# A planned instruction order that puts attention ahead of the MLP on TensorE

## The chip, the cores and the metric

The kernel runs on one core of a Trainium2 chip. The metric is device time in microseconds for one execution, and the median of several runs is compared. A profile of one execution shows TensorE (PE, with its weight loads PEld), VectorE (DVE), ScalarE (ACT), GpSimd (POOL) and SyncE (SP), which issues most of the transfers.

## The reference, cut to what matters

Three layers follow each other on 3072 tokens (4 batches of 768): a linear recurrence ("attention"), an MLP, and a mixture of experts.

```
for t in range(S):                      # attention, 8 heads of 48, complex decay a
    S = a[t] * S + outer(k[t], v[t])    # real part is read
    y[t] = q[t] @ S.real
h = x @ w_in;  g = elu(h);  x = g @ w_out                 # MLP, 384 -> 2048 -> 384
logits = x @ w_gate + log1p(exp(x @ w_noise)) * noise     # routing, 8 experts
top2, weights = best two experts of each token
out[token] += weight * (relu(x[token] @ w1[e]) @ w2[e])   # experts, 384 -> 1024 -> 384
```

## The kernel before, in words

The recurrence is worked in 6 chunks of 128 time steps. A chunk has two units (12 in all, of two batches each). Attention for one unit: magnitudes and angles of the decay (`nat_a`), sums of angles over time by a triangular matmul (`tp<-tri`), cosines and sines on ACT (`X`), cumulative products (`E`), scaled keys and queries (`KK`, `X`), their scores `sc`, masked scores `P` on DVE, the output `py`, copied to `yr`, transposed and split into a high and a low part `xh`, `xl` (two buffers each, so two units of it can exist), and, for the next chunk, transposed keys `KT` and the state update `pu`. The sines need another ACT table than the exponentials, so each block of them has a table load before and after it.

The MLP for one unit works on `xh`, `xl` in 8 steps. A step has 18 matmuls into `ph` (first layer, high and low parts, 256 columns), five instructions on ACT and DVE (`ge`, `gh`, `gl`), and 12 matmuls into `y2` (second layer, shown as `y`). `ph` has two buffers. After the two units of a chunk the routing picks two experts for each token: small DVE and ACT instructions on one tile `route`, then matmuls into `pr` that rank the tokens of each expert, then 8 scatters from POOL's queue into `table`. `pr` uses the same two buffers as `ph`, in the order in which the program was written, so a `ph` tile that was written down after `pr` can't start before it.

The expert part then reads `slots` from the table (SP), gathers token rows `xr` (POOL), transposes them (`mtp`), and runs `mph` and `mpo` for expert after expert.

The order on each engine isn't the written one. `arrange` builds a list of all instructions with estimated costs and dependences and plays a list schedule: whichever engine is free first takes, of its ready instructions, the one with the best priority. It then fixes that order on every engine. Before, the priority is the length of the estimated chain that still hangs on the instruction (`tail`). Engines run their instructions in that fixed order; semaphores make them wait. The written order, set by the table `PAR` (class, start and length in units of time), matters through buffers, as with `pr`. Everything from the check on (`cut`, the end of routing and the experts) keeps its written order.

Of the kernel before, what the change touches and what calls it, by code (L numbers as in the profile page):

```python
# [10 lines left out]
F32 = mybir.dt.float32  # L11
# [10 lines left out]
PAR = {'EARLY': 8, 'x': (-0.25, 0.3), 'w': (0.15, 1.0), 'p': (-0.25, 0.6), 't': (-0.2, 0.0), 'o': (-0.1, 0.2), 'm': (0.35, 0.15), 's': (0.1, 0.0), 'k': (1.0, 0.0), 'v': (0.1, 0.0), 'a': (1.2, 0.55), 'b': (1.45, 0.35), 'f': (2.1, 0.95), 'r': (2.9, 1.05), ('pr', 'p'): 1.0, ('o', 1): 0.3, ('b', 2): -0.3, ('m', 's', 7): -0.1, ('t', 2): -0.3, ('b', 's', 8): 0.1, ('p', 's', 4): 0.2, ('a', 11): -0.15, ('b', 11): -0.3, ('b', 's', 11): 0.4, ('o', 11): -0.15, ('b', 's', 6): -0.1, ('a', 1): -0.15, ('p', 1): -0.3, ('p', 's', 3): 0.1, 'z': (0.9, 0.0), 'q': (0.3, 0.0), ('b', 's', 1): 0.1, ('p', 0): 0.3, ('o', 2): -0.3, ('a', 's', 0): -0.3, ('a', 's', 4): -0.5, ('a', 's', 6): 0.1, ('a', 's', 2): 0.1, ('k', 0): 0.15, ('o', 's', 0): -0.2, ('a', 0): -0.3, ('b', 's', 4): -0.2, ('b', 's', 0): 0.2, ('b', 's', 7): -0.3, ('m', 11): -0.3, ('b', 's', 2): 0.0, ('pr', 't'): -0.5, ('f', 2): 0.15, ('b', 's', 10): 0.3, 'ring': '0000001111', 'bufs': (2, 2), ('t', 0): -0.45, ('a', 's', 3): 0.1, ('p', 's', 0): -0.1, ('f', 0): -0.15, ('pr', 'q'): 0.5, ('b', 's', 12): -0.2, ('t', 1): 0.3, ('b', 's', 5): 0.3, ('m', 's', 0): 0.2, ('pr', 'f'): -0.5, ('pr', 'x'): -1, 'fs': 0, ('q', 0): 0.45, ('a', 's', 1): 0.1, ('k', 1): 0.15, ('o', 0): -0.3, ('m', 's', 8): -0.2, ('q', 2): -0.3, ('v', 0): 0.15, ('p', 2): 0.15}  # L22


def arrange(tc):


    nc = tc.nc
# [223 lines left out]
    pr = {h: -tail[h] if h < cut else 1e9 + h for h in heads}  # L252
# [6 lines left out]
    mode, dma, zeros = None, 0.0, []  # L259
# [22 lines left out]
    while done < len(heads):  # L282
# [15 lines left out]
        p, h = heapq.heappop(now[e])  # L298
        st = t
# [36 lines left out]
def tile_kernel(ctx, tc, q, k, v, a_re, a_im, w_in, w_out, w_gate, w_noise, noise, w1, w2, qp, kp, vp, ap,  # L336
# [33 lines left out]
    xs = dram.tile([N, Dm], F32, name="xs") if dbg is None else dbg["xs"]  # L370
# [512 lines left out]
    def route(lg, noi, tok, nt, small, psm, put):  # L883
# [45 lines left out]
        tt(both, oh[:, :, 0], oh[:, :, 1], op=OP.add)  # L929
        pr = psm()  # L930
# [26 lines left out]
    def r_pieces(c):  # L957
        def f():
            noi = wf.tile([128, B, E], F32, name="noi", tag="noi", bufs=1)
            nc.sync.dma_start(noi, noise.rearrange("(b t) e -> t b e", b=B)[c * L:(c + 1) * L])  # L960
            route(LG[c], noi, tokm[:, c, :], B, wf,
                  lambda: psf.tile([128, B + 1, E], F32, name="pr", tag="ph", bufs=2), put_row)
        return [(1.0, f)]
# [131 lines left out]
    def place(cls, u, pieces):  # L1095

        tot = sum(w for w, _ in pieces) or 1.0
        t0, ln = PAR[cls]
        if cls not in "wx":
            t0 += u + PAR.get((cls, u), 0.0)  # L1100
        t = 0.0
        for k, (w, f) in enumerate(pieces):
            t += w
            ev[cls, u, k] = [t0 + ln * t / tot + PAR.get((cls, "s", k), 0.0), f]

# [111 lines left out]
    settle(rules)  # L1217
    events = [(t, n, f, u, c) for n, ((c, u, k), (t, f)) in enumerate(ev.items())]
# [13 lines left out]
    for t, _, f, tag, cls in sorted(events, key=lambda e: e[:2]):  # L1232
        tc.cur_priority = int((t + 4 - PAR.get(("pr", cls), 0.0)) * SCALE)
        if dbg is not None:
            dbg["labels"].append((int(nc.get_next_instruction_name().split("-")[1]), f"{cls}.{kind(f)}:{tag}"))
# [3 lines left out]
    if dbg is not None and dbg.get("p1"):  # L1239
# [102 lines left out]
    def redo():  # L1342
# [79 lines left out]
        with tc.tile_pool(name="gf", bufs=1) as gf, tc.tile_pool(name="gfp", bufs=1, space=PSUM) as gp:  # L1422
# [20 lines left out]
            with tc.For_i(0, N, 128) as r:  # L1443
# [36 lines left out]
                route(lg, noi, tk, 1, gf, lambda: gp.tile([128, 2, E], F32, name="gfpr"), put)  # L1480
# [68 lines left out]
```

## Time and profile before

| | |
|---|---|
| median of 3 runs | 1263.4 us (1262.4 to 1264.09) |
| profiled execution, its own time | 1264.73 us |
| its span in the profile | 1262.9 us |
| PE busy | 1164.5 us, 92% |
| DVE busy | 791.2 us, 63% |
| ACT busy | 649.5 us, 51% |
| mean granted TensorE clock | 0.966 |

The start, to about 160 us, loads and splits weights. From 160 to about 767 us attention and MLP run interwoven; from then the experts run. In the middle part the same pattern comes back about every 112 us, once for each chunk.

### The profile page before, as it was taken

The page shows a single profiled execution, that of the slowest core. Times are in us where ns is not written, and L with a number is a line of the kernel's source. Part 1 is how long each engine was busy: PE and PEld are TensorE (multiplying, and loading weights), DVE is VectorE, ACT ScalarE, POOL GpSimd, SP SyncE. Part 2 cuts the span into 40 slices and gives each one's busy share as a digit, 9 for nine tenths or more (in the row PEclk, how much of TensorE's full clock was granted, in tenths as well). Part 3 has the DMA queues.
Part 4 walks back from the last instruction along what each step waited for, and adds up shares of the span by engine and source line. Part 5 has one row for each costly group of instructions (what it writes and reads, how often), then busy time and mean ns, then how long its engine had stood idle before and what let it go on. Part 6 is the DMA issues. An engine that isn't in the chain of part 4 may idle for free.

```text
span 1262.9 us, 22761 instructions
## 1 busy us (share of the span) xinstructions
PE 1164.5 (92%) x8821; PEld 1077.0 (85%) x8821; DVE 791.2 (63%) x1782; ACT 649.5 (51%) x1299; POOL 243.2 (19%) x265
## 2 busy tenths in 40 slices
PE   4786999889899989999997999799999999999997
PEld 3464989889898988989897998789898989898996
DVE  5799986996898699679848466343443343443221
ACT  6777766685766678576745374232323232332111
POOL 2110000030020003001100502433424242424222
PEclk9597999999999999999998999899999999999999
DMA  6455502211121111112100234343434342423111
GB/s 216 124 154 175 181 28 66 64 48 36 61 74 34 56 50 57 45 56 79 35 26 20 53 106 120 99 125 103 127 97 126 94 133 84 134 83 109 36 44 34
DMA packets 64309, 107.05 MB, mean 85 GB/s; under 512 B 19967, under 2 KB 46310, under 8 KB 64192
## 3 DMA queue, kind: packets, MB, share of 16 engines
q1 hardware_dynamic: 50096, 65.65, 17.5%
q0 software_dynamic: 14096, 39.86, 10.4%
q8 instruction: 71, 1.16, 0.4%
q14 instruction: 46, 0.38, 0.1%
HBM read 86.98 MB, written 20.70 MB: 85 GB/s over the span
## 4 chain that ended last, share of the span: by engine, by line
PE 59%; DVE 24%; ACT 10%; issue 4%; DMA 1%; POOL 0%; another core or an unknown queue 0%; SPq 0%; POOLq 0%; ACTq 0%; DVEq 0%
PE mpo L1073 17%; PE mph L1051 17%; PE y L859 8%; PE ph L835 8%; DVE E L618 2%; DVE ge L841 2%; DVE KK L677 2%; DVE X L686 2%; PE mtp L1036 1%; DVE gl L845 1%; DVE Sc L755 1%; ACT L562 1%; DVE P L768 1%; PE sc L764 1%; PE tp L587 1%
## 5 line engine op out<-in xcount | busy, mean ns | idle before, releaser
L1053 ACT ACTIVATE egh<-mph 128x320 fp32r<-128x320 f32 (+1 forms) x128 | 66.3, 518 | 231.6 <-PE mpo L1073 131.9
L951 POOL DMA_INDIRECT table<-route x48 | 55.1, 1148 | 613.1 <-DVE route L945 542.3
L1073 PE MATMUL mpo<-weh,egh 128*128 128x384 f32 (+1 forms) x448 | 151.7, 339 | 0.0
L1073 PE MATMUL mpo<-weh,egl 128*128 128x384 f32 (+1 forms) x448 | 151.6, 338 | 0.0
L1073 PE MATMUL mpo<-wel,egh 128*128 128x384 f32 (+1 forms) x448 | 151.2, 337 | 0.0
L859 PE MATMUL y<-woh,gh 128*128 128x400 f32 x384 | 141.0, 367 | 0.5 <-ACT yo L871 0.5
L859 PE MATMUL y<-woh,gl 128*128 128x400 f32 x384 | 132.6, 345 | 0.0
L859 PE MATMUL y<-wol,gh 128*128 128x400 f32 x384 | 131.4, 342 | 0.0
L1078 DVE SCALAR_TENSOR_TENSOR ac<-mpo,slots,ac 128x384 f32<-128x384 f32 (+1 forms) x49 | 30.2, 617 | 160.8 <-PE mpo L1073 160.8
L1054 DVE SCALAR_TENSOR_TENSOR egl<-mph,egh 128x320 fp32r<-128x320 f32 (+1 forms) x128 | 75.2, 587 | 87.1 <-ACT egh L1053 59.4
L835 PE MATMUL ph<-xh,wih 128*128 128x256 f32 x576 | 106.4, 294 | 4.0 <-DVE ge L841 3.9
L1004 ACT ACTIVATE weh<-raw 128x384 fp32r<-128x384 f32 x128 | 65.4, 523 | 86.6 <-PE mpo L1073 60.0
L835 PE MATMUL ph<-xl,wih 128*128 128x256 f32 x576 | 101.3, 285 | 2.8 <-DVE xl L802 2.7
L835 PE MATMUL ph<-xh,wil 128*128 128x256 f32 x576 | 100.7, 284 | 0.0
L1081 POOL DMA_INDIRECT out_dram<-ac,slots x56 | 55.4, 989 | 234.2 <-DVE ac L1078 210.5
L845 DVE TENSOR_TENSOR gl<-ge,gh 128x512 fp32r<-128x512 f32 x96 | 65.8, 689 | 49.3 <-ACT gh L844 48.6
L835 PEld LDWEIGHTS ph<-xh,wih 128*128 128x128 f32 x576 | 87.9, 191 | 5.6 <-PE sc L764 3.6
L844 ACT ACTIVATE gh<-ge 128x512 fp32r<-128x512 f32 x96 | 60.4, 629 | 61.4 <-PE y L859 49.4
L839 ACT ACTIVATE ge<-ph 128x512 f32<-128x512 f32 x96 | 57.2, 596 | 63.6 <-DVE gl L845 47.1
L835 PEld LDWEIGHTS ph<-xl,wih 128*128 128x128 f32 x576 | 83.0, 191 | 3.8 <-DVE xl L802 3.8
L841 DVE SCALAR_TENSOR_TENSOR ge<-ge,ph 128x512 f32<-128x512 f32 x96 | 65.6, 683 | 32.2 <-ACT ge L840 27.3
L1005 DVE TENSOR_TENSOR wel<-raw,weh 128x384 fp32r<-128x384 f32 x128 | 69.3, 556 | 25.8 <-ACT weh L1004 18.8
(207 smaller groups left out, 2861.7 us busy)
## 6 DMA issues: line engine op xcount, KB each, us to landing
raw<-in_moe_w_dram SPq DMA_DIRECT2D x128, 192.0 KB
nat_a<-in_a_rows_dram SPq DMA_DIRECT2D x24, 512.0 KB
raw<-in_moe_w_in_dram POOLq DMA_DIRECT2D x16, 384.0 KB
raw<-in_moe_w_out_dram POOLq DMA_DIRECT2D x16, 384.0 KB
q<-in_q_pairs_dram SPq DMA_DIRECT2D x24, 256.0 KB
k<-in_k_pairs_dram SPq DMA_DIRECT2D x24, 256.0 KB
vt<-in_v_rows_dram SPq DMA_DIRECT2D x24, 192.0 KB
out_dram<-zero SPq DMA_DIRECT2D x24, 192.0 KB
```

Of the source, the lines that this page charges most:

```text
L835: mm(ph[:, j, :], w[:, z, :], x[:, z, :], start=n == 0, stop=n == 3 * KD - 1)
L839: act(e, ph, AF.Relu, scale=-1.0)
L841: stt(e, e, -1.0, ph, op0=OP.add, op1=OP.max)
L844: act(gh, e, AF.Copy)
L845: tt(gl, e, gh.bitcast(F32), op=OP.subtract)
L859: mm(d["y"][i], g[:, j, i * L:(i + 1) * L], w, start=s == 0 and j == 0 and n == 0, stop=s == NS - 1 and j == 1 and n == 2)
L1004: act(w[0], raw, AF.Copy)
L1005: tt(w[1], raw, w[0].bitcast(F32), op=OP.subtract)
L1051: mm(ph[:, :n], w[:, z, :], x[:, z, :], start=k == 0, stop=k == 3 * KD - 1)
L1053: act(gs[0][:, f, :n], ph[:, :n], AF.Relu)
L1054: stt(gs[1][:, f, :n], ph[:, :n], 0.0, gs[0][:, f, :n].bitcast(F32), op0=OP.max, op1=OP.subtract)
L1073: mm(po[:m], x[:, f, o:o + m], w, start=k == 0, stop=k == 3 * FE - 1)
```

## The change

`arrange` gets two new rules. First, a PE instruction before `cut` that touches neither a `ph` nor a `y2` tile gets 30000 added to its priority, so that attention (and weight splitting, ranking and `mtp`) is taken ahead of any MLP matmul that is ready at that moment. Second, a sine block on ACT (an instruction with an estimated cost over 900 ns, after 150 us) is taken only when PE has at least 5000 ns of ready work by the estimate; after 12000 ns of waiting it is taken all the same. The routing becomes a generator in two pieces, `choose` (up to the two experts) and `rank` (from `pr` on), and for all chunks but the last it is written down later, in the midst of the next unit's MLP (in `PAR`, 'r' goes from (2.9, 1.05) to (2.5, 1.05), and `place` adds the chunk's number and 1). An empty list `ORDER` and some unused debugging lines change nothing.

```diff
-    pr = {h: -tail[h] if h < cut else 1e9 + h for h in heads}
+    pr = {}
+    for h in heads:
+        mlp = any(x[4] and x[0].startswith(("ph_", "y2_")) for x in acc[h])
+        pr[h] = 1e9 + h if h >= cut else -tail[h] - (30000 if eng[h] == "PE" and not mlp else 0)
...
+    hold = 5000
...
+        if hold and e == "Activation" and step[h] > 900 and t > 150000:
+            if free["PE"] - t + sum(work[x] for _, x in now["PE"]) + sum(work[x] for r, _, x in cand["PE"] if r < t) < hold:
+                waited.setdefault(h, t)
+                if t < waited[h] + 12000:
+                    nxt = min([free[x] for x in E if free[x] > t] + [t + 500])
+                    heapq.heappush(cand[e], (max(nxt, t + 100), p, h))
+                    continue
...
         tt(both, oh[:, :, 0], oh[:, :, 1], op=OP.add)
+        yield
         pr = psm()
...
-        return [(1.0, f)]
+        return [(1.0, choose), (0.3, rank)]
...
+        if cls == "r" and u < NC - 1:
+            t0 += u + 1
```

The instructions are the same in number and kind on all five engines; only their order differs. PE's order is the same up to the first MLP matmul (about 127 us in the trace) and again from the last 48 `y` matmuls on.

PE, just ahead of the ranking of chunk 2 (units count from 0, so chunk 2 has units 4 and 5). Before, this is the end of attention for unit 6, and no MLP matmul is among the rows:

```order
L786 MATMUL py<-vt,P 64x48 x2
L800 MATMUL tp<-ident,yr 128x128 x3
L711 MATMUL tp<-ident,KK 128x128 x8
L800 MATMUL tp<-ident,yr 128x128 x3
L725 MATMUL pu<-vt,KT 64x48 x16
L764 MATMUL sc_5438<-X,KK 128x128
L587 MATMUL tp<-tri,nat_a 128x128 x4
L933 LDWEIGHTS before
```

The changed kernel ahead of the same ranking; this is attention for unit 7, and `ph` and `y_5157`, `y_5158` belong to the MLP of unit 6:

```order
L801 MATMUL py<-vt,P 64x48 x2
L850 MATMUL ph<-xh,wih 128x256 x3
L850 MATMUL ph<-xl,wih 128x256 x3
L850 MATMUL ph<-xh,wil 128x256 x3
L815 MATMUL tp<-ident,yr 128x128 x3
L726 MATMUL tp<-ident,KK 128x128 x4
L874 MATMUL y_5157<-woh,gh 128x400
L874 MATMUL y_5157<-wol,gh 128x400
L874 MATMUL y_5157<-woh,gl 128x400
L874 MATMUL y_5158<-woh,gh 128x400
```

Before, the MLP of unit 5 has just been used up there, and the first matmul of unit 6's stands behind the ranking. Now attention is one unit further on at the same ranking, MLP matmuls of unit 6 stand between its steps, and 27 more `ph` matmuls of unit 6 follow the ranking.

PE, the first transposes for the experts (`mtp`), in the MLP of unit 10 (`y_7818` before, `y_7756` now). Before:

```order
L835 MATMUL ph<-xh,wih 128x256 x3
L835 MATMUL ph<-xl,wih 128x256 x3
L835 MATMUL ph<-xh,wil 128x256 x3
L1036 MATMUL mtp<-ident,xr_8129 128x128 x3
L1036 MATMUL mtp<-ident,xr_8131 128x128 x3
L859 MATMUL y_7818<-woh,gh 128x400
```

Now:

```order
L874 MATMUL y_7757<-woh,gl 128x400
L1059 MATMUL mtp<-ident,xr_8129 128x128 x3
L850 MATMUL ph<-xh,wih 128x256 x3
L850 MATMUL ph<-xl,wih 128x256 x3
L850 MATMUL ph<-xh,wil 128x256 x3
L1059 MATMUL mtp<-ident,xr_8131 128x128 x3
L850 MATMUL ph<-xh,wih 128x256 x3
L850 MATMUL ph<-xl,wih 128x256 x3
L850 MATMUL ph<-xh,wil 128x256 x3
L1059 MATMUL mtp<-ident,xr_8133 128x128 x3
```

What moved is the distance from the last ranking of chunk 4 (`pr`), on whose table rows the gathers wait: before, 198 `ph`, 84 `y` and 86 attention matmuls stand between its last matmul and the first `mtp`; now 81 `ph` and 42 `y` matmuls and nothing else. Behind the last attention matmul before the experts stood 153 `ph` and 150 `y` matmuls; now 351 and 276.

## Rows read from the trace of the kernel before

**Rows 1.** The page: span, and busy time of the engines.

```profile
span 1262.9 us, 22761 instructions
PE 1164.5 (92%) x8821; PEld 1077.0 (85%) x8821; DVE 791.2 (63%) x1782; ACT 649.5 (51%) x1299; POOL 243.2 (19%) x265
```

**Rows 2.** Busy time by stretch; behind the colon the stretch's length, then engines, clock.

```profile
160.00:222.80 62.80, 59.72 (x534) 57.45 (x534) 47.46 (x95) 42.70 (x83) 0.00 (x0) 1.00 0.16 47
222.80:334.68 111.88, 104.10 (x1036) 100.02 (x1035) 91.60 (x217) 77.45 (x151) 9.70 (x8) 0.98 0.18 53
...
446.49:558.29 111.80, 104.33 (x1036) 100.12 (x1035) 91.53 (x217) 77.19 (x149) 9.69 (x8) 0.98 0.18 53
558.29:674.60 116.31, 108.80 (x1083) 104.45 (x1081) 89.44 (x215) 70.70 (x131) 10.59 (x8) 0.97 0.16 43
674.60:730.00 55.40, 46.75 (x431) 45.51 (x432) 34.13 (x85) 25.85 (x43) 15.80 (x22) 0.91 0.17 48
```

**Rows 3.** Waits of PE from 222.8 to 674.6 us: total, times, longest.

```profile
PE tp L711 <- ACT KT L713: 12.0, 8, 2.4
PE py L786 <- DVE P L768: 9.1, 8, 1.8
PE ph L835 <- DVE ge L841: 3.9, 7, 0.8
PE ph L835 <- DVE xl L802: 2.7, 4, 0.7
PE pr L933 <- DVE route L929: 1.6, 2, 1.4
```

**Rows 4.** Timeline of PE, one chunk's stall: start, duration, [idle before, releaser].

```profile
452.37 0.32 PE L786 MATMUL py<-vt,P 128*64 128x48 f32 x4 [1.74 <-DVE P L768]
...
457.40 0.66 PE L711 MATMUL tp<-ident,KK 128*128 128x128 f32 x4 [0.83 <-ACT KT L713]
...
462.55 0.17 PE L933 MATMUL pr<-route,before 128*128 128x8 bf16 x1 [1.36 <-DVE route L929]
```

**Rows 5.** Busy time and granted clock by stretch, around two stalls.

```profile
450.00:452.30 2.30, 0.63 (x13) 0.43 (x12) 2.30 (x5) 2.27 (x4) 0.00 (x0) 1.00 0.00 0
452.30:454.60 2.30, 2.23 (x52) 2.23 (x52) 2.24 (x5) 0.49 (x3) 0.00 (x0) 0.66 0.28 46
454.60:457.40 2.80, 1.97 (x13) 1.48 (x11) 2.65 (x12) 1.76 (x6) 0.00 (x0) 0.67 0.34 126
...
683.00:688.40 5.40, 5.40 (x27) 5.40 (x27) 4.52 (x12) 1.72 (x3) 0.00 (x0) 0.50 0.10 36
```

**Rows 6.** Timeline of PE, the ranking of chunk 4.

```profile
682.50 0.17 PE L933 MATMUL pr<-route,before 128*128 128x8 bf16 x1 [7.30 <-DVE route L929]
```

**Rows 7.** Timeline of ACT, a sine block and the first instruction behind it.

```profile
494.56 1.28 ACT L562 ACT_TABLE_LOAD   x1
...
498.91 1.28 ACT L569 ACT_TABLE_LOAD   x1
500.21 0.63 ACT L844 ACTIVATE gh<-ge 128x512 fp32r<-128x512 f32 x1
```

**Rows 8.** Timelines: from ranking to first scatter, chunk 5.

```profile
777.45 0.17 PE L935 MATMUL pr<-route,ones 128*128 128x8 bf16 x1
779.53 1.02 POOL L951 DMA_INDIRECT table<-route  x1 [58.05 <-DVE flags L1272]
```

**Rows 9.** Timelines, chunk 4: first and last scatter, slots, first gather, first mtp.

```profile
700.73 0.96 POOL L951 DMA_INDIRECT table<-route  x1 [93.68 <-DVE route L945]
...
709.57 0.96 POOL L951 DMA_INDIRECT table<-route  x1 [0.31 <-issue]
711.91 0.39 SPq L1020 DMA_DIRECT2D slots<-table  x1
715.40 1.06 POOL L1031 DMA_INDIRECT xr<-xs,slots  x1 [1.92 <-DMA slots<-table]
734.81 0.82 PE L1036 MATMUL mtp<-ident,xr 128*128 128x128 f32 x6
```

**Rows 10.** Timelines: a later gather, and the mtp that waits for it.

```profile
795.01 1.05 POOL L1031 DMA_INDIRECT xr<-xs,slots  x1 [3.67 <-issue]
...
798.15 0.55 PE L1036 MATMUL mtp<-ident,xr 128*128 128x128 f32 x3 [1.40 <-DMA xr<-xs,slots]
```

**Rows 11.** Chain that ended last: start, length, what; one MLP step.

```profile
396.13 2.17 PE y L859 x12
398.30 2.14 PE ph L835 x18
```

More of the change, by code (lines that the diff above doesn't have):

```diff
@@ L25, in arrange @@
+ORDER = []
 def arrange(tc):
@@ L258, in arrange @@
     now = {e: [] for e in E}
-    mode, dma, zeros = None, 0.0, []
+    hold = 5000
+    mode, dma, zeros, waited = None, 0.0, [], {}
+    work = {h: sum(step[z] for z in members[h]) for h in heads}
     order = []
@@ L369, in tile_kernel @@
     nc.scalar.preload_act_table_set("natural_log_exp_and_others")
-    xs = dram.tile([N, Dm], F32, name="xs") if dbg is None else dbg["xs"]
+    xs = dram.tile([N, Dm], F32, name="xs")
     table = dram.tile([E * RS, 2], I32, name="table")
@@ L957, in r_pieces, with choose, rank @@
     def r_pieces(c):
-        def f():
+        g = []
+        def choose():
             noi = wf.tile([128, B, E], F32, name="noi", tag="noi", bufs=1)
             nc.sync.dma_start(noi, noise.rearrange("(b t) e -> t b e", b=B)[c * L:(c + 1) * L])
-            route(LG[c], noi, tokm[:, c, :], B, wf,
-                  lambda: psf.tile([128, B + 1, E], F32, name="pr", tag="ph", bufs=2), put_row)
-        return [(1.0, f)]
+            g.append(route(LG[c], noi, tokm[:, c, :], B, wf,
+                           lambda: psf.tile([128, B + 1, E], F32, name="pr", tag="ph", bufs=2), put_row))
+            next(g[0])
+        def rank():
+            for _ in g[0]:
+                pass
+        return [(1.0, choose), (0.3, rank)]
     def clear_table(pool):
@@ L1217, in tile_kernel @@
     settle(rules)
+    if ORDER:
+        for z, t in zip(ev.values(), ORDER):
+            z[0] = t / 5000.0
+        settle(rules)
     events = [(t, n, f, u, c) for n, ((c, u, k), (t, f)) in enumerate(ev.items())]
@@ L1231, in tile_kernel @@
             events.append((te, len(events), lambda f=f, n=n: e_weight(0, f, n), "m", "M"))
-    for t, _, f, tag, cls in sorted(events, key=lambda e: e[:2]):
+    for t, n, f, tag, cls in sorted(events, key=lambda e: e[:2]):
         tc.cur_priority = int((t + 4 - PAR.get(("pr", cls), 0.0)) * SCALE)
         if dbg is not None:
-            dbg["labels"].append((int(nc.get_next_instruction_name().split("-")[1]), f"{cls}.{kind(f)}:{tag}"))
+            dbg["labels"].append((int(nc.get_next_instruction_name().split("-")[1]), n, cls, tag, kind(f)))
         f()
     tc.cur_priority = (NU + 10) * SCALE
-    if dbg is not None and dbg.get("p1"):
+    if False:
         sm.close()
@@ L1479, in put @@
                                                  out_offset=bass.IndirectOffsetOnAxis(ap=idx, axis=0))
-                route(lg, noi, tk, 1, gf, lambda: gp.tile([128, 2, E], F32, name="gfpr"), put)
+                for _ in route(lg, noi, tk, 1, gf, lambda: gp.tile([128, 2, E], F32, name="gfpr"), put):
+                    pass
                 ts(tk, tk, 128.0, None, op0=OP.add)
```

2 lines of the change are left out of this document (1 added, 1 removed).

## The prediction

> **What bounds the kernel now.** I read the page first: TensorE is busy 92% of a span of 1262.9 us, VectorE 63% and ScalarE 51% [rows 1]. That is a mean over parts with different limits, so the next view is the busy time by stretch. From 222.8 to 674.6 us one pattern repeats four times, once a chunk; the third of these is alike to the second, which I left out. In each TensorE is idle for 7.8 us (111.88 less 104.10, 111.80 less 104.33; the last 116.31 less 108.80), while VectorE is busy 91.6 of 111.9 us and ScalarE 77 [rows 2]. So TensorE is nearest to its limit, VectorE has some 20 us of room in a chunk. Behind these four, 674.6 to 730 has 8.65 us of TensorE's idle time, and ahead of them 160 to 222.8 has 3.1 [rows 2].
>
> The view of waits says what the idle time of the four chunks is made of: 12.0 us for transposed keys that ScalarE copies, 9.1 for masked scores that VectorE makes, 1.6 for the ranking, all of them attention's chain or routing, and 6.6 for the MLP's own tiles, together 29.3 us [rows 3]. The timeline of one chunk shows where: within 12 us TensorE waits 1.74, 0.83 and 1.36 us [rows 4]. These stand in the piece of the order in which attention's steps follow each other without an MLP matmul between. They are not stalls of an engine that lacks speed, but of one that has nothing else ready: the MLP of the unit before is done, and the next needs `xh`, `xl` from the end of this very chain.
>
> Each such cluster costs twice. The granted clock behind the first gap is 0.66 and 0.67 for 5.1 us, after 2.30 us in which TensorE was busy 0.63 [rows 5]. TensorE was busy 4.2 us of these, and a third of that is 1.4 us a chunk. The ranking of chunk 4 is the longest wait of all, 7.30 us [rows 6], with matmuls of the next MLP queued behind it that need nothing from it but their turn in the `ph` buffers; then TensorE runs 5.4 us at 0.50 [rows 5], which is the lower of the two levels, 1.2 GHz, and loses 2.7 us.
>
> **The change part by part.** No instruction is added or removed, so nothing has a price of its own; the sum is made of gaps that close and gaps that open.
>
> *Attention first (A).* In the changed order attention runs about one unit ahead of the MLP, as far as two `xh` buffers let it, and MLP matmuls stand between its steps. The work that now hides attention's chain is the MLP of the unit before: a step of it is 2.14 and 2.17 us on TensorE [rows 11], eight steps a unit. In the changed order the second half of each unit's attention resumes just behind the last `ph` matmul of the MLP two units back, after a stretch of MLP alone. So attention waits for TensorE's MLP, no longer the other way, and a chain that is late has that stretch to catch up. The idle time of the four chunks is 30.5 us (7.8, 7.7, 7.5 and 7.5) [rows 2]. What can remain? Attention's matmuls are now put exactly where the planner thinks that they become ready, so each lateness of the chip against the planner is a stall with MLP matmuls queued behind it. The nearest row is the sine block: from the first table load to the next instruction it holds ScalarE 5.65 us [rows 7], and the rule asks for 5.0 us of work on TensorE, so at the end of each block TensorE lacks 0.65 us and then about the 0.63 us of ScalarE's next instruction, 1.3 us, twice a chunk. With 0.2 us for the rest I take 2.8 us a chunk. The gain is 30.5 less 11.2, 19.3 us; the bounds are 0 (all gaps come back elsewhere) and 30.5.
>
> *Clock (B).* 1.4 us in each of four chunks is 5.6. Gaps of 1.3 us are shorter than the 2.30 us one that pulled the clock down, but not absent; I take half, 2.8, between 0 and 5.6.
>
> *The hold on the sines.* It delays ScalarE's longest block until TensorE has work; what it saves is in A. It can cost: the sines wait up to 12 us, and scores of the next unit wait for them. The stretch of MLP alone hides that; if that cover is gone, the delay is in rival 2.
>
> *Routing split and shifted (C).* `pr` now takes its turn among the `ph` buffers in the midst of the next unit's MLP, so the chain of small VectorE instructions has several MLP steps of 4.3 us [rows 11] to end in. The wait of 7.30 us goes, and the slow 5.4 us behind it: 10.0 us, at least 7.3. The 1.6 us in the four chunks [rows 3] is already in A.
>
> *Early stretch (D).* Of 3.1 us from 160 to 222.8 I take 1.0; attention has no lead yet. Bounds 0 and 3.1.
>
> *The first transposes for the experts (E).* This is the loss. Chunk 4 is ranked later, and its table rows must land before the first gather. The chain: last ranking matmul to first scatter 2.1 us, with VectorE little loaded [rows 8]; first to last of eight scatters 8.84; to the slots' load 2.34; to the first gather 3.49 [rows 9]; from a gather to the transpose that waits for it 3.14 [rows 10]. Together 19.9 us. In the old order 52 us lay between ranking and `mtp` (682.50 to 734.81) [rows 6, 9]. In the new one 81 `ph` and 42 `y` matmuls do, 81/18 times 2.14 and 42/12 times 2.17 [rows 11], 17.2 us. And `mtp` is among the instructions that are taken first, so the MLP matmuls that could fill the gap stand behind it. That is a new wait of 2.7 us, with some 0.3 for VectorE's MLP instructions among the ranking's, and 1.4 us of slow clock as after the gap of similar length: 4.4 us lost, bounds 2.4 and 7. The next three `mtp` are 1.1 us of matmuls and 0.3 of their own apart, gathers come about every 1.3, so they add nothing.
>
> The MLP that is left when attention ends, 351 and 276 matmuls in place of 153 and 150, costs nothing: it is the same work later, and a stretch of MLP alone keeps TensorE busy without a gap [rows 11]. The experts' order is the same.
>
> The sum: 19.3 + 2.8 + 10.0 + 1.0 - 4.4 = 28.7 us. The profiled execution took 1264.7 us, so 1236.0; the runs' median, 1263.4, is 1.3 lower than that execution, which gives 1234.7, **1235 us**. The ends of the terms give 1264.7 - 46.8 = 1218 and 1264.7 - 0.3 = 1264 on the same footing, 1217 and 1263 for the median.
>
> **The rivals.**
>
> *1. The gaps move and don't close.* Attention's chain runs through VectorE and ScalarE; the order of these two isn't governed by the new rule. For it: VectorE is busy 82% of a chunk [rows 2], and attention must now be done sooner. By the order, the MLP alone behind the last attention grows by 198 `ph` and 126 `y` matmuls, 46 us [rows 11], and VectorE's work for attention must fit into that much less time. Against it: 20 us of its time are free in each chunk. Then A, B and D are nothing, and C less E is left, 5.6 us: about 1258. One rule of the Trainium skill points this way: "Perfetto Trace Analysis", section on optimization strategy, says that a gap that keeps repeating on the engine that should be full can mean too few buffers for the next tile. By that rule a new order gains nothing here until `xh` or `ph` get a third buffer, and the sum would be 1258; the trace agrees only for the ranking, which waits for its turn in the buffers, while the larger waits end on a copy or a masked score [rows 3], on data, not on a buffer.
>
> *2. Slower: in-order stalls.* A unit's attention has about 15 groups of matmuls, 30 a chunk, each now at its earliest place, with the MLP queued behind it. If each stalls by as much as an average MLP wait now, 0.6 us (6.6 us in 11 times [rows 3]), that is 18 us a chunk in place of 7.6: 42 us more over four chunks, less the 5.6 of C and E: about 1300. It decides from the point at which a group stalls 0.3 us on the mean: 9 us a chunk, so that 1.4 us more in each of four chunks eats the 5.6. Against it: the small waits now stand once or twice a chunk at places where filler was to be had, not at all of them, and lateness doesn't pile up over the stretch of MLP alone.
>
> *3. Nearly all gaps close*, and the clock stays up: 1264.7 - 46.8, about 1217.
>
> *4. No change*: what A gains, late groups take, within 2.5 us of 1263.4. I count a difference under 0.2%, 2.5 us, as one that these measurements can't tell from none.
>
> **How the numbers follow.** Forecast (A between 11 and 26, others near their values; 1225 to 1245): 0.60. Rival 1 (1248 to 1261): 0.18, of which 0.02 lies within the 2.5 us. Rival 2: 0.11. Rival 3: 0.07. Rival 4: 0.04. Faster: 0.60 + 0.16 + 0.07 = 0.83; same 0.06; slower 0.11. The range from 1219 to 1257 holds the forecast, most of rival 1 and most of rival 3, and leaves out rival 2, rival 4 and the ends, about 2 in 10.
>
> **What would show it.** Right: between about 200 and 640 us TensorE idle 3 us or less per 104 us of its work, the waits for `KT` and `P` at under half of [rows 3], no wait of `pr` over 1 us, the span of the experts the same, and a new wait of `mtp` for `xr` of about 3 us some 40 us before `mph` starts. Wrong for rival 1: the same waits in sum at other steps, VectorE busy over 95% where they stand. Wrong for rival 2: many waits of 0.3 to 1 us at `sc`, `py`, `KT` and `yr`, with a granted clock under 0.9 in the chunks. If `pr` still waits some us, the shift was too small and C is lost; if `mtp` waits 10 us, the ranking's chain was longer than from these rows.

## The result, and the profile after

The changed kernel takes 1252.4 us (median of 4 runs, 1249.1 to 1253.4), the kernel before 1262.9 us in the runs beside it: a ratio of 0.9915, 95% interval 0.989 to 0.9939. It is 10.5 us faster. The forecast was 28.4 us less than before: the direction was right and the time lies inside the range, but the gain is well under half of what the sum had.

The page of the changed kernel, span and busy time as in [rows 1]:

```profile
span 1251.6 us, 22832 instructions
PE 1160.8 (93%) x8821; PEld 1070.9 (86%) x8821; DVE 786.7 (63%) x1782; ACT 648.9 (52%) x1299; POOL 234.4 (19%) x265
```

Busy time of the changed kernel in the stretches of [rows 2], then up to the first expert matmul (`mph`), which starts at 757.0 us; behind the colon the stretch's length, then PE, PEld, DVE, ACT and POOL, and the granted clock:

```profile
160.00:222.80 62.80, 56.09 (x561) 53.01 (x560) 57.39 (x122) 42.69 (x82) 0.00 (x0) 0.97 0.17 55
222.80:334.68 111.88, 104.71 (x1125) 98.31 (x1123) 101.15 (x243) 86.02 (x173) 8.55 (x8) 1.00 0.21 68
334.68:446.49 111.81, 106.36 (x1106) 102.45 (x1105) 95.14 (x233) 78.93 (x156) 7.67 (x8) 0.98 0.18 55
446.49:558.29 111.80, 104.46 (x1030) 99.96 (x1029) 91.35 (x218) 76.91 (x149) 7.83 (x8) 0.97 0.17 53
558.29:674.60 116.31, 112.38 (x1028) 108.99 (x1027) 78.11 (x173) 62.34 (x105) 11.39 (x18) 1.00 0.10 31
674.60:757.00 82.40, 79.59 (x548) 78.34 (x547) 44.78 (x112) 46.47 (x94) 12.19 (x12) 1.00 0.25 73
160.00:757.00 597.00, 563.60 (x5385) 541.04 (x5384) 467.92 (x1096) 393.36 (x755) 47.62 (x54) 0.99 0.18 55
```

The same view of the kernel before, whose first `mph` starts at 766.5 us:

```profile
160.00:766.50 606.50, 564.28 (x5392) 544.20 (x5392) 470.51 (x1092) 396.64 (x757) 55.47 (x54) 0.98 0.19 54
```

Length less PE's busy time is TensorE's idle time. From 160 us to the experts it falls from 42.2 to 33.4 us, and the busy time by 0.7 us; that is the 9.5 us by which the experts start earlier, and the other 1.8 us of the span lie behind. The four chunks' stretches hold 23.9 us of idle time (7.2, 5.5, 7.3 and 3.9) where there were 30.5. These stretches are the same in time, not in work: the changed order does 4289 matmuls in the four, the old one 4191. Only the stretch from 160 us to the experts compares nearly the same work (5385 and 5392).

What these 23.9 us are made of, in the view of waits of the changed kernel over the same 222.8 to 674.6 us (total, times, longest), against [rows 3]:

```profile
PE ph L850 <- DVE ge L856: 6.8, 10, 2.1
PE pr L949 <- DVE route L944: 6.3, 3, 2.7
PE y L874 <- DVE gl L860: 3.1, 4, 0.9
PE py L801 <- DVE P L783: 1.9, 2, 1.2
PE sc L779 <- DVE sx L744: 1.8, 2, 1.0
PE sc L779 <- DVE X L683: 1.6, 2, 0.9
PE sc L779 <- DVE X L684: 0.8, 1, 0.8
PE tp L815 <- DVE xl L817: 0.7, 1, 0.7
PE tp L602 <- ACT nat_a L581: 0.6, 1, 0.6
```

The 12.0 us for `KT` are gone and the 9.1 for `P` are 1.9, as foreseen. In their place TensorE waits longer for the MLP's own tiles (`ge` 6.8 for 3.9, `gl` 3.1 for nothing), 4.2 us at the scores `sc`, and 6.3 at the ranking for 1.6. Three single waits, from the timeline of TensorE: at the triangular matmul in the early stretch, at the ranking of a chunk, and the new one at the first transpose for the experts:

```profile
215.17 0.38 PE L602 MATMUL tp<-tri,nat_a 128*128 128x128 f32 x1 [3.94 <-ACT nat_a L581]
...
395.19 0.17 PE L949 MATMUL pr<-route,before 128*128 128x8 bf16 x1 [2.44 <-DVE route L944]
...
715.11 0.55 PE L1059 MATMUL mtp<-ident,xr 128*128 128x128 f32 x3 [2.45 <-DMA xr<-xs,slots]
```

Where a long wait comes from is seen on ScalarE and VectorE, here around a sine block of the changed kernel, with the MLP matmul that waits behind it (TensorE's row last):

```profile
511.37 1.28 ACT L577 ACT_TABLE_LOAD   x1
512.67 1.06 ACT L577 ACTIVATE X<-X 128x1024 f32<-128x1024 f32 x1
...
515.73 1.28 ACT L584 ACT_TABLE_LOAD   x1
517.03 0.63 ACT L855 ACTIVATE ge<-ge 128x512 f32<-128x512 f32 x1
```
```profile
514.80 1.23 DVE L692 TENSOR_TENSOR KK<-KK,X 128x1024 f32<-128x1024 f32 x1 [6.91 <-ACT X L578]
...
517.78 1.22 DVE L701 TENSOR_TENSOR X<-X,E 128x1024 f32<-128x1024 f32 x1
518.93 0.68 DVE L856 SCALAR_TENSOR_TENSOR ge<-ge,ph 128x512 f32<-128x512 f32 x1
```
```profile
519.66 0.62 PE L850 MATMUL ph<-xh,wih 128*128 128x256 f32 x3 [2.05 <-DVE ge L856]
```

ScalarE is held from 511.37 to 517.0, 5.6 us, as in [rows 7], and its part of the MLP's `ge` ends at 517.66. But VectorE's part starts only at 518.93. VectorE's order is fixed too: it stood 6.91 us for these sines, with the attention instruction `KK` at the head of its queue, and then worked off six attention instructions before `ge`. So TensorE stands 2.05 us. From 160 to 760 us VectorE's stops for the sines at `KK` are 25.2 us, where they were 3.0; without the hold (below) the view of waits doesn't list them. They are no price by themselves: the run with routing, hold and corrected estimates has 26.6 us of them and is 44.4 us faster than before.

In the list of estimated costs from which `arrange` fixes the order, only the second table load stands, the one that the program asks for. The order was made for a block 1.28 us shorter. How much of this one wait comes from that was not worked out.

### The profile page after: what moved, and what is told of

Read it like the earlier page. It is cut to its first block, busy times and chain, and to the rows that moved or that the text cites. A ratio compares the mean times of both kernels' runs of the same rounds, so it can differ in the third digit from the quotient of the medians.

```text
span 1251.6 us, 22832 instructions
## 1 busy us (share of the span) xinstructions
PE 1160.8 (93%) x8821; PEld 1070.9 (86%) x8821; DVE 786.7 (63%) x1782; ACT 648.9 (52%) x1299; POOL 234.4 (19%) x265
## 4 chain that ended last, share of the span: by engine, by line
PE 51%; DVE 25%; issue 14%; ACT 6%; DMA 2%; POOL 2%; POOLq 0%; SPq 0%; DVEq 0%; ACTq 0%
PE mpo L1096 18%; PE mph L1074 17%; PE ph L850 4%; PE y L874 4%; DVE gl L860 2%; DVE ge L856 2%; DVE E L633 2%; DVE X L701 2%; PE mtp L1059 1%; DVE P L783 1%; DVE KK L692 1%; DVE Sc L770 1%; PE sc L779 1%; ACT L577 1%; POOL table L967 1%
## 5 line engine op out<-in xcount | busy, mean ns | idle before, releaser
L967 POOL DMA_INDIRECT table<-route x48 | 47.1, 981 | 593.4 <-DVE route L961 275.4
L854 ACT ACTIVATE ge<-ph 128x512 f32<-128x512 f32 x96 | 57.2, 596 | 63.5 <-DVE gl L860 39.7
L856 DVE SCALAR_TENSOR_TENSOR ge<-ge,ph 128x512 f32<-128x512 f32 x96 | 65.5, 683 | 33.6 <-ACT ge L855 32.3
L1028 DVE TENSOR_TENSOR wel<-raw,weh 128x384 fp32r<-128x384 f32 x128 | 69.3, 555 | 23.9 <-ACT weh L1027 22.1
L850 PEld LDWEIGHTS ph<-xh,wil 128*128 128x128 f32 x576 | 83.8, 193 | 0.0
```

Source lines behind the costliest of these rows:

```text
L850: mm(ph[:, j, :], w[:, z, :], x[:, z, :], start=n == 0, stop=n == 3 * KD - 1)
L856: stt(e, e, -1.0, ph, op0=OP.add, op1=OP.max)
L967: st = nc.gpsimd.indirect_dma_start(out=table[:, :], out_offset=bass.IndirectOffsetOnAxis(ap=idx, axis=0), in_=row, in_offset=None)
L1028: tt(w[1], raw, w[0].bitcast(F32), op=OP.subtract)
```

## The experiments

Theory 1 is the prediction's: attention first closes the chunks' idle time, routing is worth little. Theory 2, formed from the two traces, is called "late order" in the expectations. By it `arrange` puts each instruction where it is ready by its estimates; these are too short, so the chip runs behind at place after place. The parts of the change then have no price of their own, only one that depends on the lateness that they meet. "The replay" is an estimate: each kernel's fixed order played again with its own list of dependences and durations from the trace (1.28 us for the missing table load, some 12 ns more for each VectorE instruction, 1.265 us from one indirect transfer to the next). Where the expectations give its figure, it missed by 1 to 14 us, so it is no proof of theory 2. A third reading, the rival to both in the second group, is that buffers or VectorE's pace hold the rest of the idle time.

Times are medians; the difference is to the kernel before in the same group of runs (1264.8, 1263.1, 1262.4, 1261.8 and 1262.7 us).

**Parts of the change, with the old estimates.** Edits to the changed kernel: the priority without its 30000 (no lead), `hold = 0` (no hold), and the routing back in one piece at its old place:

```diff
-        pr[h] = ... -tail[h] - (30000 if eng[h] == "PE" and not mlp else 0)
+        pr[h] = ... -tail[h] - 0
...
-    hold = 5000
+    hold = 0
...
-        return [(1.0, choose), (0.3, rank)]
+        return [(1.0, lambda: (choose(), rank()))]
...
-        if cls == "r" and u < NC - 1:
-            t0 += u + 1
```

(and `'r': (2.9, 1.05)` again). Attention first alone:

> Attention first alone; the sines aren't held and the routing stays whole and early, as before the change. The theory of the prediction (attention first closes the chunks' idle time, terms A, B and D, without the new wait E): about 20 us faster than before, ratio near 0.984. The theory formed from the two traces (late order): both orders run some 30 us behind the estimates from which they were fixed, since these leave out 1.28 us of table load at each block of sines and some ns at each VectorE instruction; attention is put at the earliest places, where it is just as late as before, and the ranking still blocks the `ph` buffers. An estimate, from replaying this fixed order with the durations of the trace: within 2 us of before, ratio 0.998 to 1.003, with TensorE idle about as long as before between 160 us and the experts.

Measured: 1274.1 us, 9.4 slower, ratio 1.0075 (1.0054 to 1.0096). Both were wrong, theory 1 by 29 us. The idle time isn't closed:

```profile
160.00:776.40 616.40, 572.29 (x5346) 548.74 (x5347) 467.50 (x1093) 391.79 (x755) 49.06 (x54) 0.98 0.18 53
```

It is 44.1 us, 1.9 more than before, and the busy time grew by 8.0 for 46 fewer matmuls; why that grew was not followed up. The routing alone:

> The routing in two pieces and later, alone; priorities as before and no hold. The prediction: C less E at most, 5.6 us faster than before (ratio 0.9955), since without attention first the chunks' idle time stays. Late order: it is this part that lets later MLP matmuls past the ranking, so fillers stand ready all through a chunk; the replay with the durations of the trace gives about 17 us faster than before (ratio near 0.987), and faster than the whole change by some us, with no wait of the ranking over 2 us.

Measured: 1256.1 us, 8.7 faster, 0.9922 (0.9898 to 0.9946): the bulk of what the whole change gave, and no wait of the ranking over 0.5 us. The replay's 17 us were too many, and it isn't faster than the whole change, as theory 2 had it. Without the hold:

> The whole change without the hold on the sines. The prediction counts the hold as part of A: without it at most a few us slower than the whole change. Late order: the hold puts the sines where TensorE has 5 us of work, and so covers the table load that the estimates leave out; without it the replay gives about 7 us slower than the whole change, near the time before (ratio to before 0.997 to 1.003), with more waits of TensorE, each short.

Measured: 1269.2 us, 4.4 slower than before, 1.0037 (1.0022 to 1.0052), so the hold is worth 15 us to the changed kernel, more than either theory had. The view of waits from 160 us to the experts, first row, and one of these nine waits on TensorE, then ScalarE ahead of it:

```profile
PE y L874 <- ACT yo L886: 15.1, 9, 2.8
```
```profile
570.35 0.45 PE L874 MATMUL y<-woh,gh 128*128 128x400 f32 x1 [2.80 <-ACT yo L886]
```
```profile
568.43 1.28 ACT L584 ACT_TABLE_LOAD   x1
569.73 0.18 ACT L885 ACTIVATE lg<-y 128x16 f32<-128x16 f32 x1
569.81 0.49 ACT L886 ACTIVATE yo<-y 128x384 f32<-128x384 f32 x1
```

The last MLP's result `yo` has to leave its buffer before the next `y` matmul; its copy stood behind a sine block. In the changed kernel this wait isn't there at all. Without the routing's shift:

> Attention first and the hold, with the routing whole and early as before. The prediction: A, B and D stay, C and E go: about 23 us faster than before (ratio 0.982). Late order: attention goes ahead but the MLP matmuls that should fill behind it wait for their turn behind the ranking in the `ph` buffers, and the hold then delays sines while TensorE is idle; the replay gives about 11 us slower than before (ratio near 1.009), with long waits at the ranking or behind the held sines.

Measured: 1281.9 us, 17.2 slower, 1.0134 (1.0111 to 1.0158), where theory 1 had 23 faster and theory 2 some 11 slower. The first row of its waits is the ranking:

```profile
PE pr L949 <- DVE route L944: 11.6, 4, 5.0
```

The two parts left, run later:

> The change without attention first, with the old estimates: routing split and shifted, and the hold. The prediction would lose A and B here, 22 us, and so be slower than before. By the runs with corrected estimates, the hold alone and attention first alone each do as well as both: the hold and the routing alone are then within 6 us of the changed kernel or faster (the replay: 2 us faster), so 1244 to 1256 us.

Measured: 1251.3 us, 10.5 faster, 0.9911 (0.9894 to 0.9928), the same as the whole change (10.5), where theory 1 had it slower than before. So attention first, at its full lead, adds nothing to the measured gain that these runs can tell. Without the hold it even costs: 4.4 slower with it, 8.7 faster with the routing alone.

> The hold on the sines alone: attention isn't taken first, the routing is whole and early, the estimates are old. If the hold has a worth of its own, 3 us or more faster than before. If it only repairs what attention first does to ScalarE's queue, nothing is left to repair here, and sines that are held while the MLP waits behind the ranking cost time: 3 to 10 us slower than before (the replay: 5).

Measured: 1266.9 us, 4.2 slower, 1.0027 (1.0013 to 1.004), as expected from a hold that only repairs what attention first does. So of the three parts the routing's shift is the one that gained by itself.

**The estimates.** The list of costs corrected in three places, without any change to the work:

```diff
+    for h in members:
+        if str(getattr(ins[h], "func", "")).endswith(("Sin", "Arctan")):
+            step[h] += 1283
+            dur[h] += 1283
...
-            return s, s + 92
+            return s + 12, s + 92
...
-                return (1050, 0) if any(x[5] for x in acc[n]) else (1000, 0)
+                return (1265, 0) if any(x[5] for x in acc[n]) else (1000, 0)
...
-                fin[z] = max(st + 1900, dma + 600)
+                fin[z] = max(st + (2500 if step[z] == 1265 else 1900), dma + 600)
```

> The changed kernel, whole, but the order is fixed with one more estimate: the first sine or arctangent of a run costs 1283 ns more, for the table load that the trace shows ahead of it (1.28 us). The instructions are the same; only their order moves. Late order: the lateness that piles up at each of the blocks goes, the waits of TensorE at sc, at the triangular matmul and at ge shrink, and the time falls by 4 to 9 us against the changed kernel (an estimate, 7 from replaying both orders with the durations of the trace): near 1245 us. The rival (the idle time that is left is a matter of buffers and of VectorE's pace, which no order moves): within 2.5 us of the changed kernel.

> The changed kernel with only the VectorE estimate corrected (12 ns more for each instruction). The three corrections together gave 27 us, the table load alone 3 (1249.4 against 1252.4). If the many small errors of VectorE are the main cause of the lateness: 8 to 15 us faster than the changed kernel, 1237 to 1245 us. If each correction alone is worth little because the others' lateness remains (the replay has 6 for this one): 3 to 7 us.

> The changed kernel with only the indirect transfers' estimates corrected. If VectorE's stops at scatters (4.8 us in the changed kernel) and the late first gathers are a main cause: 6 to 10 us faster than the changed kernel, 1242 to 1246 us, both waits gone. If not: under 4 us, only the wait of mtp (2.6 us) less.

> As the run before, and two more estimates corrected by the trace: 12 ns more for each VectorE instruction, and 1265 ns in place of 1050 between indirect transfers with a later landing (2500 in place of 1900 ns). Late order: a further 8 to 16 us, so 12 to 24 us faster than the changed kernel, 1228 to 1240 us, the wait of mtp for xr (2.6 us) gone, and less than half of TensorE's idle time from 160 us to the experts left (33.4 us now). The rival: no more than 2.5 us.

Measured, table load alone: 1249.4 us, 13.7 faster than before, 0.9871 (0.9848 to 0.9894). That is 3.2 more than the changed kernel gained (0.989 to 0.9939), under the expected 4 to 9 and not clear of noise. VectorE alone: 1242.7, 19.1 faster, 8.6 more than the changed kernel, as much as was expected of a main cause. Indirect transfers alone: 1243.6, 18.1 faster, 7.6 more; from 700 us on the waits of `mtp` for `xr` fell from 9.1 to 2.6 us there, less but not gone. All three: 1225.4, 37.6 faster than before, 0.9705 (0.9688 to 0.9721), 27.1 more than the changed kernel, where the three single gains sum to 19.4 and 12 to 24 were expected. For most of the idle time the rival falls: nothing but the order moved, and buffers and VectorE's work are the same. This run's stretch to the experts, and the one ahead of it, then the changed kernel's ahead:

```profile
160.00:728.00 568.00, 550.24 (x5291) 531.33 (x5290) 454.20 (x1074) 383.67 (x740) 55.64 (x54) 0.99 0.18 57
```
```profile
0.00:160.00 160.00, 116.11 (x865) 92.51 (x866) 142.44 (x329) 127.33 (x270) 21.82 (x46) 0.91 0.52 171
```
```profile
0.00:160.00 160.00, 117.75 (x771) 90.95 (x772) 132.98 (x307) 120.23 (x256) 22.14 (x46) 0.85 0.51 168
```

Its idle time is 17.8 us in place of 33.4, 53%, where less than half was expected to be left. The other half of the gain wasn't expected: 13.4 us less of busy time is left behind 160 us. Ahead of it, where weights are split, 94 more matmuls are done in the same time; at the mean of 0.105 us (563.60 by 5385) that is some 10 us of it, an estimate. Then the old order with the same corrections, and parts of the change on top:

> The kernel before the change, with the three estimates corrected and nothing else. Late order says that much of what the corrected estimates gave the changed kernel (27 us) lies in lateness that the old order has too: 12 to 20 us faster than before (an estimate, 18 from the replay with the trace's durations), ratio 0.984 to 0.990. If the estimates matter only where attention is put at its earliest places, they give the old order 5 us or less.

Measured: 1230.8 us, 31.5 faster, 0.975 (0.9738 to 0.9763), far over the expected 12 to 20. The old order lost at least as much to its estimates as the new one. About half of it is idle time (26.4 us are left of 42.2). Nearly as much, 13.4 us, is busy time: 841 matmuls are done ahead of 160 us in place of 765. The rest lies behind the start of the experts:

```profile
160.00:737.30 577.30, 550.92 (x5316) 534.24 (x5316) 463.93 (x1078) 380.95 (x740) 48.99 (x54) 0.98 0.19 57
```

> The routing split and shifted alone, priorities as before the change and no hold, with the same three estimates corrected. If attention first and the hold only make up for wrong estimates, they aren't needed once the estimates are right: this is then as fast as the changed kernel with all estimates corrected, or up to 5 us faster. If attention first has a worth of its own, as the prediction had it (A), this is 10 us or more slower than that one.

> The changed kernel with the three estimates corrected, without the hold on the sines. If the hold's worth of 17 us in the changed kernel came from covering a table load that the estimates left out, it is worth 3 us or less now (the replay has it at nothing): 1223 to 1229 us. If the hold has a worth of its own (it keeps sines from starting while TensorE has little ready), 1235 us or more.

> The changed kernel with the three estimates corrected, attention not taken first, the hold kept. Against the changed kernel with corrected estimates (1225 us) this is what attention first is worth when the estimates are right: the routing alone with corrected estimates took 1236, so 8 to 12 us slower if attention first is what made that difference; within 3 us if the hold did. The replay has it at 3.5 us slower.

> The changed kernel with the three estimates corrected, the routing whole and early as before. In the kernels with the old estimates the shift of the routing is worth 10 us alone and 29 us under attention first and hold (1281.9 against 1252.4). If the MLP matmuls that wait behind the ranking in the `ph` buffers are the cause, right estimates don't help it: 15 to 30 us slower than with the shift, 1240 to 1255 us (the replay: 22). If the shift only gave time for lateness, it is worth 5 us or less now.

Measured, with corrected estimates:

| parts | median | to before | ratio (95%) |
|---|---|---|---|
| none | 1230.8 | -31.5 | 0.975 (0.9738 to 0.9763) |
| routing | 1236.4 | -26.6 | 0.9778 (0.9756 to 0.9799) |
| routing, hold | 1217.9 | -44.4 | 0.9649 (0.9637 to 0.9662) |
| routing, first | 1216.6 | -45.8 | 0.9636 (0.9622 to 0.965) |
| all (the change) | 1225.4 | -37.6 | 0.9705 (0.9688 to 0.9721) |
| first, hold | 1255.7 | -6.7 | 0.9948 (0.9934 to 0.9962) |

For the routing alone the second reading came out: it is 11 us slower than all parts together, and attention first has a worth of its own on top of it. Without the hold, and without attention first, both readings were wrong: each of these two is faster than all parts together, not slower or equal. The routing alone now costs some 5 us, by intervals that just overlap; attention first and the hold are each worth 18 to 19 us on top of it, and together less than either, by 7 to 8 us. The shift of the routing under both is worth 31 us, as its expectation had from the buffers, so that reading held.

Could the corrected orders be better by luck? Each of the six combinations was also run with the old estimates, and each is faster with the corrected ones, by 18 to 50 us (none 31.5, routing 17.9, routing and hold 34.0, routing and first 50.2, all 27.1, first and hold 23.8). Six times in six is hard to put down to luck. But estimates moved the other way were not tried, and the lateness itself, planned against traced start, isn't shown here. What the hold costs beside attention first, up to the experts, is 2.3 us of idle time and 5.0 us of busy time for the same matmuls, at a lower granted clock:

```profile
160.00:720.70 560.70, 545.23 (x5290) 526.21 (x5289) 454.26 (x1074) 382.95 (x740) 49.19 (x54) 1.00 0.20 58
```

That is the kernel without the hold, at 1.00, against 550.24 (x5291) at 0.99 with it.

**The lead's size.** In place of 30000:

> Attention's lead in the priority 6000 in place of 30000, routing split and shifted, no hold, with the old estimates. With the full lead and old estimates this was 4.7 us slower than before, the routing alone 9.9 faster. If the full lead was only too large, the mild one is as fast as the routing alone or faster: 1245 to 1256 us. If it is the old estimates that make any lead lose, it lies near the full lead: 1262 us or more. The replay puts it 7 us faster than before.

> A version meant to beat both kernels: corrected estimates, routing split and shifted, no hold, and attention's lead in the priority 6000 in place of 30000, so that it goes ahead only of MLP matmuls that are less than 6000 ns of estimated chain more urgent. If attention first is best as a mild preference (the run without any lead took 1236, with 30000 1217): 1208 to 1217 us. If the full lead is what gains: 1220 us or more.

Measured, old estimates, no hold: 1247.4 us, 15.3 faster than before, 0.987 (0.9852 to 0.9889), against 4.4 slower with the full lead and 8.7 faster with none. So the full lead was too large; a mild one gains some 7 us over the routing alone even with the old estimates. Corrected estimates, no hold: 1211.5 us (1209.3 to 1212.4), 50.2 faster, 0.9595 (0.9581 to 0.9609), inside the 1208 to 1217 of the mild preference, the fastest of all and 39.7 more than the changed kernel has. Its idle time up to the experts is 11.6 us, at a clock of 1.00:

```profile
160.00:716.00 556.00, 544.42 (x5293) 527.38 (x5292) 459.48 (x1074) 380.64 (x740) 49.49 (x54) 1.00 0.20 58
```

**A stop on VectorE.** In the run with the routing alone, TensorE's second longest wait (4.43 us) led back to this row on VectorE: an instruction that writes the next chunk's table rows, taken early in the order since nothing else hinders it, waits until the scatters have read the last ones. The MLP's `ge` is queued behind:

```profile
494.25 0.17 DVE L960 TENSOR_SCALAR route<-tokm 128x8 int32<-128x8 f32 x1 [4.18 <-DMA table<-route]
...
498.48 0.68 DVE L856 SCALAR_TENSOR_TENSOR ge<-ge,ph 128x512 f32<-128x512 f32 x1
```
```profile
499.31 0.77 PE L850 MATMUL ph<-xh,wih 128*128 128x256 f32 x3 [4.43 <-DVE ge L856]
```

A tile of their own in two buffers for rows and positions:

```diff
+        rows = small.tile([128, 6 * nt], F32, name="rows", tag="rows", bufs=2).bitcast(I32)
+        po = rows[:, :2 * nt].rearrange("p (a b) -> p a b", b=2)
...
-        row = new("row", [nt, 2, 2], I32)
+        row = rows[:, 2 * nt:].rearrange("p (a b c) -> p a b c", b=2, c=2)
```

> The routing split and shifted alone, and the table rows that the scatters read get a tile of their own in two buffers. In the run with the routing alone VectorE waits 8.9 us in two stops (the longest 4.7) for scatters to finish before it may write the rows of the next chunk, with the MLP's ge behind it. If these stops cause the longest waits of TensorE there (5.05 and 4.43 us for ge), the two shrink to about 2 us like the others (2.05), and the time falls by 4 to 6 us against routing alone. If the block of sines ahead of ge on ScalarE alone causes them, the time stays within 2 us and the waits stay.

Measured: 1245.5 us, 17.5 faster than before, 0.9865 (0.9846 to 0.9885), 8.8 more than the routing alone where 4 to 6 were expected. The two longest waits of TensorE, 5.05 and 4.43 us, are now 2.79 and 2.84, not quite the expected 2:

```profile
382.26 0.55 PE L850 MATMUL ph<-xh,wih 128*128 128x256 f32 x1 [2.79 <-DVE ge L856]
...
491.48 0.98 PE L850 MATMUL ph<-xh,wih 128*128 128x256 f32 x3 [2.84 <-DVE ge L856]
```

The stretch to the experts, first this run, then the routing alone:

```profile
160.00:746.80 586.80, 558.20 (x5381) 543.08 (x5378) 471.70 (x1088) 386.91 (x753) 58.16 (x54) 0.99 0.19 56
```
```profile
160.00:759.00 599.00, 565.38 (x5393) 548.17 (x5392) 472.79 (x1091) 388.37 (x755) 56.09 (x54) 0.98 0.19 55
```

Against the routing alone the idle time falls by 5.0 us (33.6 to 28.6) and the busy time by 7.2 (565.4 to 558.2). So the stop was behind a good part of both long waits; what is left of them stands behind a sine block: VectorE now stops 2.53 us there until the sines end, with `ge` queued behind. The buffer on top of the changed kernel wasn't tried.

## Why the prediction was wrong, step by step

**The step that failed is term A**, at "What can remain? ... I take 2.8 us a chunk". That attention's waits for `KT` and `P` would go was right: 19.2 us of them went, which is the size of A. But what remains was taken from one lateness, 0.65 us at the end of a sine block, and came to 23.9 us in place of 11.2. That is 6.0 us a chunk where 2.8 was taken, and A is 6.6 us, not 19.3. The text itself said that "each lateness of the chip against the planner is a stall with MLP matmuls queued behind it", and then it priced one of them. The mechanism was wrong too: that MLP matmuls between attention's steps close the gaps. Attention first by itself left 44.1 us of idle time in place of 42.2 and was 9.4 us slower, and without it the change is as fast, so the 6.6 us aren't its gain. What kept TensorE idle was not lack of filler alone, but in good part an order made from durations that the chip doesn't have: with its estimates corrected, the old order loses 15.8 of its 42.2 us of idle time with no new rule.

**B** (2.8) was 0.7, if all by which the busy time up to the experts fell is put down to the clock. **D** (a gain of 1.0) was a loss of 3.6: 6.7 us of idle time from 160 to 222.8 us for 3.1, of which 3.94 is the one wait for the arctangent, the last of a sine block.

**C and E** were near. From 674.6 us to the experts the idle time falls from 8.65 to 2.8 us: the 7.30 us of [rows 6] are gone, and of the 2.8 the wait of `mtp` is 2.6 (the sum had 2.7), 42 us ahead of `mph` (40 were foretold). Its 1.4 us of slow clock didn't come; the clock there is 1.00. What C missed is that later rankings wait elsewhere, 6.3 us in the chunks, where "no wait of `pr` over 1 us" was foretold. C less E was 5.6 us in the sum; the idle time there fell by 5.8. Together A, B and D are 3.7 us where the sum had 23.1. The experts' span, foretold to stay the same, is 1.8 us shorter.

**The hold** had no term of its own: its saving was counted in A, and its cost was to be hidden by the stretch of MLP. Alone it costs 4.2 us; with attention first at full lead and old estimates it gives back 15.

**Rival 1** came closer than the forecast. It had the band in which the time fell (1248 to 1261), its A, B and D of nothing are nearer to 3.7 than 23.1 is, and its words "the same waits in sum at other steps" describe most of it (23.9 of 30.5 us). Its other sign was seen as well. Over whole stretches VectorE is busy 91% at most (57.39 of 62.80 us), but not where the waits stand; here the last 2 us of the three longest in the chunks, two at the ranking and one at `ge`:

```profile
393.19:395.19 2.00, 0.00 (x0) 0.00 (x0) 1.94 (x15) 0.72 (x2) 0.00 (x0) 1.00 0.02 1
504.16:506.16 2.00, 0.00 (x0) 0.00 (x0) 1.94 (x15) 0.72 (x2) 0.00 (x0) 0.91 0.11 10
517.66:519.66 2.00, 0.00 (x0) 0.00 (x0) 1.97 (x4) 0.52 (x1) 0.47 (x1) 1.00 0.64 16
```

In the 17 waits on VectorE of 0.6 us or more in the chunks, each with the 2 us ahead of it, VectorE is busy 52.4 of 54.0 us, 97%. So at these places VectorE's queue is what TensorE waits for. That it is VectorE's pace doesn't follow: with the same VectorE work in a better order the idle time fell to 11.6 us. The rule beside it, that a repeating gap can mean too few buffers (the Trainium skill, "Perfetto Trace Analysis", section on optimization strategy), isn't borne out for `xh` and `ph`: with both as they were, idle time fell to 11.6 us. It did hold for a buffer that I hadn't looked at, the table rows. **Rival 2**, slower by in-order stalls, has the direction of attention first at full lead by itself (9.4 us, a quarter of its price of some 37), but not its mechanism: up to the experts it has only 1.9 us more of idle time.

What stays open: which of the three corrections does more in the loading stretch (alone none brings over 811 matmuls to 160 us, together 865); why the busy time grew under attention first alone; and why attention first and the hold together are slower than each alone, beyond the slower clock.

## What to carry over

When an order is fixed from estimated costs, compare estimated and traced durations first, instruction by instruction: a missing 1.28 us, 12 ns here and there and a late transfer were worth 31.5 us of 1263, three times what the new rules gave. Price a new rule of order together with the lateness that it will meet; here parts that lost with wrong estimates gained with right ones, and two that gained were worse together. Look at VectorE's busy share in the 2 us ahead of a wait, not over a whole stretch. In a queue that runs in order, look for the unimportant instruction at the head of a long wait: an early place does harm if what it waits for is late.

## What the runs showed of the hardware that wasn't expected

A switch of ScalarE's tables took 1.28 us, and the next instruction followed at once (511.37, then 512.67); the instruction ahead of it ended at 511.36. The Trainium skill, "ScalarE: Activation LUTs", section on what a table load costs, gives 1283 ns for the load and some 1380 ns for a drain, 2.66 us a switch. The load agrees; no drain is seen here.

The indirect scatters of one chunk, eight in a row, don't keep a fixed distance. In [rows 9] first and last are 8.84 us apart, with VectorE busy 2.83 of 9.90 us. In the run with the routing alone eight such scatters took 12.0 us, from 479.31 to 491.33:

```profile
479.31 2.43 POOL L967 DMA_INDIRECT table<-route  x1 [99.92 <-DVE route L961]
...
491.33 0.96 POOL L967 DMA_INDIRECT table<-route  x1 [0.31 <-issue]
```
```profile
479.30:492.30 13.00, 12.53 (x138) 11.95 (x137) 10.76 (x22) 12.03 (x24) 10.85 (x8) 1.00 0.03 5
```

VectorE was busy 10.76 of 13.00 us there. The Trainium skill, "SBUF — State Buffer", section on who interferes with whom, says that GpSimd shares a port pair with VectorE and that a VectorE instruction with two inputs from SBUF contends with a GpSimd instruction that reads SBUF. That would fit this row, but not the next, where VectorE also ran instructions with two such inputs (`gl<-ge,gh`, `KK<-KK,k`): in the changed kernel eight scatters stood 1.26 us apart throughout, 8.83 us from first to last, with VectorE busy 7.46 of 8.90 us, nearly the same share.

```profile
614.50:623.40 8.90, 8.90 (x65) 8.90 (x64) 7.46 (x12) 4.16 (x8) 6.77 (x8) 1.00 0.04 3
```

So it isn't VectorE's busy share as such. What it is was not tried.

In these runs the kernel with long gaps paid for them twice. Taking 5.0 us of idle time out of two long and some short waits also took 7.2 us of busy time for nearly the same matmuls (5393 and 5381, at a clock of 0.98 and 0.99). The fastest kernel, with 11.6 us of idle time in waits of at most 1.3 us, ran at a granted clock of 1.00 up to the experts.
